# Loading a gated delta-rule kernel in 128-token pieces: large loads, 128-row transposes, on-chip spreads and shared PSUM banks

## The chip, the cores and the metric

One Trainium2 chip, one core. The metric is the device time of one execution in microseconds (us). The kernel before takes 416.6 us (median of 4 runs, 415.4 to 418.9). PE is the matrix engine, PEld its weight loads, DVE the vector engine, ACT the scalar engine, POOL the general engine, SP the engine that here only issues transfers. "SPq" is SP's queue. All runs are on one core; runs called slow by their own set (over 1.5% above the fastest run of the same kernel) are left out of the ratios; the medians are over all four runs.

## The reference

A recurrence over 768 tokens for 32 heads (4 batches of 8, 48 wide), then a two-layer MLP on the 3072 x 384 result.

```python
    k_n = k / (np.linalg.norm(k, axis=-1, keepdims=True) + 1e-06)
    state = np.zeros((B, H, D, D), dtype=np.float32)
# ... cut
    for t in range(S):
        kt, vt, bt = (k_n[:, :, t].copy(), v[:, :, t].copy(), beta[:, :, t, None].copy())
        readout = np.einsum('bhd,bhde->bhe', q[:, :, t], state)
        y[:, :, t] = g[:, :, t] * readout
        v_old = np.einsum('bhde,bhd->bhe', state, kt)
        state = state + bt[:, :, :, None] * np.einsum('bhd,bhe->bhde', kt, vt - v_old)
# ... cut; the MLP: h = x @ w_in; (h+1)^2/4 between -1 and 1, h above, 0 below; @ w_out
```

q, k, v and g lie in memory as [batch, head, token, 48] in float32, so that the 48 numbers of one head and one token, 192 bytes, are the longest run that stays together when tokens lie on the partitions and heads beside each other.

## The kernel before

Both kernels do the recurrence in 24 steps of 32 tokens, and four steps form a group. In a group all that does not need the state is prepared: k is normalised and scaled, k and q are transposed on PE, Gram blocks are formed, a 32 x 32 triangular system is solved for each head and step ("the solve", about 15 us of small operations on POOL, for group 0 on DVE), and two rounds of small matmuls merge the solution. Then the four steps run one after the other, each ending in the *state eviction*, a copy of the state out of PSUM by ACT. The MLP of a group runs on PE beside the next groups. The evictions are the clock by which this text tells the time: s0 is the first, s4 the first of group 1, s22 the last (the prediction and the expectations say "step 4" where this text says s4).

The loads of the kernel before, four transfers of 48 KB per tensor and step, all on SP for groups 1 to 5:

```python
    def load_step(nm, s, eng="SP", prio=0.0):
        p, c = s // 2, s % 2
        t = raw[nm](p)
        for h4 in range(4):
            a = bass.AP(tensor=src[nm].tensor, offset=src[nm].offset + h4 * S * D + s * C * D,
                        ap=[[D, C], [HS, J], [1, D]])
            e = {"SP": nc.sync, "ACT": nc.scalar}[eng]
            P(eng, 0.49, lambda h4=h4, a=a, e=e: e.dma_start(out=t[32 * h4:32 * h4 + 32, c, :, :], in_=a),
              w=[raw[nm].key(p, c, h4)], prio=prio, late=0.33)
# ... cut
    def loads(gi):
        for nm in "kqvg":
            for c in range(GS):
                load_step(nm, gi * GS + c, "SP", at((gi - 2) * GS) + (c + "kqvg".index(nm) * 0.5) * T)
```

The transposes, 64 rows at a time, and most of the small matmuls have this form (Gram blocks shown):

```python
                for jj in range(4):
                    for a in range(2):
                        for r in range(2):
                            rr = slice(64 * r, 64 * r + 64)
                            nc.tensor.matmul(tp[rr, jj, a], kq[rr, c, 4 * half + jj, a, :], i64[rr, :], ...)
# ... cut
            for j in range(J):
                for hh in range(2):
                    for r in range(2):
                        h4 = 2 * r + hh
                        rk = slice(64 * r, 64 * r + D)
                        nc.tensor.matmul(gp[32 * h4:32 * h4 + 32, j], kt[rk, j, 0, 32 * hh:32 * hh + 32], ...)
```

The order of instructions on each engine is decided when the kernel is built, by a list scheduler in the kernel. It has assumed durations for every operation (the second argument of `P`), priorities (`prio`), and one more rule that becomes important below: it counts PE instructions and plans no block of 256 sooner than 3.4 us after the one before. This is an assumption in the code; what the traces show of it comes with the profile after.

```python
            if o["n"]:
                fetch[0] += o["n"]
                while fetch[0] >= 256:
                    fetch[0] -= 256
                    fetch[1] = max(fetch[1] + 3.4, t)
                    end = max(end, fetch[1])
```

Of the kernel before, what the change touches and what calls it, by code (L numbers as in the profile page):

```python
# [22 lines left out]
class Plan:  # L23
# [3 lines left out]
    def __init__(self):  # L27
        self.ops, self.writer, self.readers = [], {}, {}
        self.banks, self.slot = {}, {}

    def add(self, eng, us, fn, r=(), w=(), prio=0.0, ninstr=0, late=0.0, take=None, give=None):
        i = len(self.ops)
        deps = set()
# [16 lines left out]
    def order(self):  # L50
# [10 lines left out]
        out = []  # L61
# [10 lines left out]
        blocked = {}  # L72
        spare = {p: list(range(n)) for p, n in self.banks.items()}
        back = []
        while len(out) < len(ops):
# [8 lines left out]
            if back and (best is None or back[0][0] <= best[0]):  # L84
                t, p, n = heapq.heappop(back)
                spare[p].append(n)
                for e, i in blocked.pop(p, ()):
                    avail[i] = max(avail[i], t)
                    heapq.heappush(ready[e][0], (avail[i], ops[i]["prio"], i))
                continue  # L90
# [8 lines left out]
            if o["take"]:  # L99
                bp = o["take"][0]  # L100
                if not spare[bp]:
                    blocked.setdefault(bp, []).append((e, i))
                    continue
                self.slot[o["take"]] = spare[bp].pop(0)
# [30 lines left out]
def kernel(  # L135
# [11 lines left out]
    nc = tc.nc  # L147
    B, H, S, D = q.shape
# [9 lines left out]
    HS = 4 * S * D  # L158
# [18 lines left out]
    raw = {nm: Ring(f"raw_{nm}", 5 if nm == "g" else 3, [128, 2, J, D], FP) for nm in "kqvg"}  # L177
    src = dict(k=k, q=q, v=v, g=g)
    ksq = Ring("ksq", 2, [128, 2, J, D], FP)
    nsq, nrm, nre, rcp, rs = (Ring(n, 2, [128, 2, J], FP) for n in ("nsq", "nrm", "nre", "rcp", "rs"))  # L180
    kqs = Ring("kq", 5, [128, 2, J, 2, 64], F16)
    vts = Ring("vt", 4, [128, 2, J, D], F16)
    kts = Ring("kt", 8, [128, J, 2, 64], F16)
    bms = Ring("bm", 2, [128, GS, J, 2, 32], F16)
# [14 lines left out]
    rls = Ring("rl", 3, [128, NT], FP)  # L199
    mxs = Ring("mx", 2, [128, NT], FP)  # L200
    r2s = Ring("r2", 2, [128, NT], FP)
    gts = Ring("gt", 23, [128, NT], F16)
# [3 lines left out]
    sb = pool.tile([128, NG, J, GS], FP, name="sb")  # L206
    sps = ps.tile([128, 2, 512], FP, name="sps")
    banks = {}
    for p, n in (("n", 3), ("h", 2), ("o", 1)):
        banks[p] = [ps.tile([128, 512], FP, name=f"ps{p}{i}") for i in range(n)]  # L210
        plan.banks[p] = n
# [7 lines left out]
    def bv(vid, *dims):  # L219

        d, stride = [], 1
        for n in reversed(dims):
            d.insert(0, [stride, n])
            stride *= n
        return _ap(banks[vid[0]][plan.slot[vid]], d)


    braw = pool.tile([128, NG, C], FP, name="braw")
    bt = pool.tile([128, NG, C], FP, name="bt")
    ones = pool.tile([128, 64], FP, name="ones")  # L230
    id32 = pool.tile([128, 32], FP, name="id32")
    i16 = pool.tile([128, 32], F16, name="i16")
    i64 = pool.tile([128, 64], F16, name="i64")
# [3 lines left out]
    eye = pool.tile([128, 2, 16, 16], FP, name="eye")  # L237
    c_half = pool.tile([128, 1], FP, name="c_half")

    def P(eng, us, fn, r=(), w=(), prio=0.0, ninstr=0, late=0.0, take=None, give=None):  # L240
        plan.add(eng, us, fn, r, w, prio, ninstr, late, take, give)

    def load_step(nm, s, eng="SP", prio=0.0):
        p, c = s // 2, s % 2
        t = raw[nm](p)
        for h4 in range(4):
            a = bass.AP(tensor=src[nm].tensor, offset=src[nm].offset + h4 * S * D + s * C * D,
                        ap=[[D, C], [HS, J], [1, D]])
            e = {"SP": nc.sync, "ACT": nc.scalar}[eng]
            P(eng, 0.49, lambda h4=h4, a=a, e=e: e.dma_start(out=t[32 * h4:32 * h4 + 32, c, :, :], in_=a),  # L250
              w=[raw[nm].key(p, c, h4)], prio=prio, late=0.33)

    def rawkeys(nm, p, cs):
        return [raw[nm].key(p, c, h4) for c in cs for h4 in range(4)]

    def beta_load():
        for h4 in range(4):
            for j in range(J):
                a = bass.AP(tensor=beta.tensor, offset=beta.offset + h4 * S + j * 4 * S,
                            ap=[[C, GS], [GS * C, NG], [1, C]])  # L260
                p = 32 * h4 + 4 * j
                P("ACT" if j % 2 else "SP", 0.33, lambda p=p, a=a, e=(nc.scalar if j % 2 else nc.sync): e.dma_start(out=braw[p:p + 4, :, :], in_=a),
                  w=[("braw", p)], prio=-50, late=0.03)

    def setup():
        P("POOL", 0.2, lambda: nc.gpsimd.memset(ones[:], 1.0), w=["ones"], prio=-100)

        def diag():
# [8 lines left out]
            for r2 in range(2):  # L277
                r = slice(64 * r2, 64 * r2 + 64)
                nc.gpsimd.affine_select(out=i64[r, :], in_=ones[r, :], compare_op=ALU.is_equal, fill=0.0,
                                        base=0, pattern=[[-1, 64]], channel_multiplier=1)  # L280
        P("POOL", 2.2, diag, r=["ones"], w=["id32", "upf", "i64"], prio=-99)
        P("DVE", 0.2, lambda: nc.vector.memset(c_half[:], 0.5), w=["c_half"], prio=-100)
        for i in range(kqs.n):
# [365 lines left out]
```

## Time and profile before

| | before |
|---|---|
| time, median (lowest to highest), us | 416.6 (415.4 to 418.9) |
| span of the profiled execution, us | 414.2 |
| first state eviction s0, us | 63.9 |
| s0 to s4 | 66.8 |
| the four groups s4 to s20 | 52.1, 52.9, 51.1, 48.9 |
| s20 to s22 | 21.3 |
| from s22 to the end | 57.2 |

These lines are from the page of the profile of the kernel before: busy time of each engine with its share of the span and its number of instructions; then PE, its granted clock and the DMA engines in 40 slices of the span, as tenths; the queues with packets, MB and the time that the packets took, as a share of 16 engines' span; and the first line of the chain of waits, which is followed back from the last instruction.

```profile
PE 264.4 (64%) x7536; PEld 158.1 (38%) x7536; DVE 216.5 (52%) x357; ACT 160.5 (39%) x277; POOL 182.2 (44%) x284
...
PE   0004145673656569985984897669983499769665
...
PEclk9999655577555666956797899968998589999989
DMA  8995444444554444544434431000100001001001
...
q1 hardware_dynamic: 104000, 22.88, 27.3%
q0 software_dynamic: 2752, 3.15, 4.8%
...
q8 instruction: 59, 0.97, 1.0%
...
PE 26%; SPq 23%; POOL 20%; issue 9%; DMA 9%; DVE 8%; ACT 3%; ACTq 0%; POOLq 0%
```

No engine is full on average. The largest thing that is not work is SP's queue, 23% of the chain. What it does is in the timeline of SP between s0 and s4 (start, duration of the stretch, line, transfer, number of issues): four issues of 48 KB take 1.9 to 3.4 us, one stretch follows the other without a pause.

```profile
72.55 3.41 SPq L250 DMA_DIRECT2D raw_k_61<-in_k_dram  x4
76.06 2.77 SPq L250 DMA_DIRECT2D raw_v_67<-in_v_dram  x4
78.87 1.93 SPq L250 DMA_DIRECT2D raw_q_64<-in_q_dram  x4
```

And these are state evictions s0, s3 and s4 in the timeline of ACT (start, duration, then what the idle time before it ended with):

```profile
63.87 0.80 ACT L494 CAST s_125<-sps 128x768 f16<-128x768 f32 x1 [0.72 <-PE sps L491]
...
81.80 0.80 ACT L494 CAST s_126<-sps 128x768 f16<-128x768 f32 x1 [0.78 <-PE sps L491]
130.72 0.80 ACT L494 CAST s_125<-sps 128x768 f16<-128x768 f32 x1
```

Between s3 and s4 the recurrence stands still for 49 us. Note also the row q8, kind "instruction": it moved 59 packets, 16,384 bytes each by the packet records. 7,536 matmuls and as many weight loads are 15,072 PE instructions, 255.5 for each of these packets; what that means is read from the trace after the change, below.

### The profile page before, as it was taken

To read this page: it belongs to the slowest core of one execution; us is meant where nothing else is said; L and a number is where in the kernel's file an instruction comes from. 1 tells how busy PE (TensorE), PEld (TensorE's weight loads), DVE (VectorE), ACT (ScalarE), POOL (GpSimd) and SP (SyncE) were. 2 spreads that over 40 slices of the span, in tenths; PEclk is the share of its full clock that TensorE was granted. 3 is DMA by queue.
4 is the path that set the end of the run, shared out by engine and by line. 5 is a ranking of instruction groups with operands and counts; after the bars stand their busy time and mean duration, and the time that the engine had idled before them with its cause. 6 is when DMAs were issued, how large, how long until landed. Compare 5 with 4: busy or idle time off the path is not lost.

```text
span 414.2 us, 16889 instructions
## 1 busy us (share of the span) xinstructions
PE 264.4 (64%) x7536; PEld 158.1 (38%) x7536; DVE 216.5 (52%) x357; ACT 160.5 (39%) x277; POOL 182.2 (44%) x284
## 2 busy tenths in 40 slices
PE   0004145673656569985984897669983499769665
PEld 0004034531225235653552464435542355425222
DVE  8303854365433364663984529472493453875530
ACT  0004013342325333452672356525453264555531
POOL 8703062244896338953489526851038420212110
PEclk9999655577555666956797899968998589999989
DMA  8995444444554444544434431000100001001001
GB/s 141 164 156 93 88 92 76 73 87 89 100 99 84 84 83 97 122 90 83 83 69 93 98 95 24 3 3 21 60 6 2 3 22 59 3 2 57 19 20 59
DMA packets 111625, 27.95 MB, mean 67 GB/s; under 512 B 106048, under 2 KB 111168, under 8 KB 111552
## 3 DMA queue, kind: packets, MB, share of 16 engines
q1 hardware_dynamic: 104000, 22.88, 27.3%
q0 software_dynamic: 2752, 3.15, 4.8%
q10 hardware_dynamic: 4800, 0.84, 1.1%
q8 instruction: 59, 0.97, 1.0%
q14 instruction: 14, 0.11, 0.1%
HBM read 25.26 MB, written 4.72 MB: 72 GB/s over the span
## 4 chain that ended last, share of the span: by engine, by line
PE 26%; SPq 23%; POOL 20%; issue 9%; DMA 9%; DVE 8%; ACT 3%; ACTq 0%; POOLq 0%
SPq L250 23%; PE pso_173 L558 11%; POOL tm_108 L401 7%; POOL lm_107 L404 7%; PE psh_172 L530 5%; DMA braw<-in_beta_dram 5%; PE psh_171 L530 3%; POOL lowl_109 L406 2%; DVE lt_106 L393 1%; DMA raw_q_64<-in_q_dram 1%; POOL r_136 L544 1%; DMA raw_k_62<-in_k_dram 1%; ACT rl_133 L533 1%; DVE mx_134 L537 1%; ACT r_137 L547 1%
## 5 line engine op out<-in xcount | busy, mean ns | idle before, releaser
L530 PEld LDWEIGHTS <-win 128*128 128x128 f16 x288 | 27.2, 105 | 64.9 <-issue 47.8
L530 PE MATMUL psh_172<-xt_129,win 128*128 128x512 f16 x69 | 23.2, 454 | 19.8 <-DVE gt_143 L549 8.1
L401 POOL TENSOR_TENSOR tm_108<-lt_106,lm_107 128x30 f32<-128x30 f16 (+7 forms) x75 | 29.9, 399 | 12.0 <-DVE lt_106 L393 6.0
L404 POOL TENSOR_TENSOR lm_107<-lm_107,tm_108 128x30 f32<-128x30 f32 (+7 forms) x75 | 29.2, 390 | 5.9
L365 PE MATMUL psn_168<-i_179,kq_87 64*64 64x64 f16 x96 | 3.3, 221 | 43.2 <-POOL kq_87 L344 36.2
L530 PE MATMUL psh_171<-xt_129,win 128*128 128x512 f16 x75 | 24.6, 443 | 4.4 <-DVE gt_149 L549 2.2
L544 POOL TENSOR_TENSOR r_136<-rl_132 128x512 f32<-128x512 f32 x8 | 9.3, 1158 | 37.6 <-ACT rl_132 L533 37.6
L530 PE MATMUL psh_172<-xt_130,win 128*128 128x512 f16 x63 | 20.3, 437 | 7.5 <-DVE gt_160 L549 1.6
L530 PE MATMUL psh_171<-xt_130,win 128*128 128x512 f16 x81 | 23.6, 402 | 2.0 <-DVE gt_151 L549 1.8
L544 POOL TENSOR_TENSOR r_136<-rl_133 128x512 f32<-128x512 f32 x8 | 8.3, 1043 | 33.0 <-ACT rl_133 L533 33.0
L365 PEld LDWEIGHTS <-kq_87 64*64 64x64 f16 x192 | 5.3, 135 | 44.3 <-POOL kq_87 L344 36.2
L533 ACT ACTIVATE rl_133<-psh_171,c_half 128x512 f32<-128x512 f32 x19 | 13.0, 685 | 18.6 <-POOL r_136 L544 10.6
L544 POOL TENSOR_TENSOR r_136<-rl_131 128x512 f32<-128x512 f32 x8 | 8.3, 1040 | 23.2 <-ACT rl_131 L533 23.2
L533 ACT ACTIVATE rl_131<-psh_172,c_half 128x512 f32<-128x512 f32 x17 | 11.7, 687 | 14.5 <-PE psh_172 L530 14.5
L533 ACT ACTIVATE rl_131<-psh_171,c_half 128x512 f32<-128x512 f32 x15 | 10.4, 690 | 16.5 <-POOL r_136 L544 11.0
L533 ACT ACTIVATE rl_132<-psh_171,c_half 128x512 f32<-128x512 f32 x18 | 12.3, 686 | 7.6 <-PE psh_171 L530 7.4
L430 PE MATMUL psn_169<-l_112,bm_105 32*32 32x32 f16 x256 | 4.3, 227 | 16.2 <-DVE l_112 L411 16.2
L533 ACT ACTIVATE rl_132<-psh_172,c_half 128x512 f32<-128x512 f32 x14 | 9.7, 690 | 12.5 <-PE psh_172 L530 12.2
L333 DVE TENSOR_REDUCE nsq_78<-ksq_76 128x16 f32<-128x768 f32 x6 | 5.7, 950 | 15.4 <-POOL ksq_76 L331 15.4
L335 ACT ACT_TABLE_LOAD x1 | 1.3, 1283 | 30.6 <-DMA raw_q_65<-in_q_dram 30.6
L430 PEld LDWEIGHTS <-bm_105 32*32 32x32 f16 x384 | 6.1, 115 | 17.9 <-issue 17.8
L411 DVE STREAM_TRANSPOSE l_112<-lowl_109 128x1024 f16<-128x1024 f16 x3 | 3.7, 1245 | 17.2 <-POOL lowl_109 L406 17.2
(473 smaller groups left out, 808.8 us busy)
## 6 DMA issues: line engine op xcount, KB each, us to landing
wout<-in_moe_w_out_dram POOLq DMA_DIRECT2D x4, 384.0 KB, 8.4
raw_v_67<-in_v_dram SPq DMA_DIRECT2D x32, 48.0 KB
raw_v_68<-in_v_dram SPq DMA_DIRECT2D x32, 48.0 KB
raw_k_63<-in_k_dram SPq DMA_DIRECT2D x32, 48.0 KB
raw_q_66<-in_q_dram SPq DMA_DIRECT2D x32, 48.0 KB
raw_v_69<-in_v_dram SPq DMA_DIRECT2D x32, 48.0 KB
out_dram<-ot_161 SPq DMA_DIRECT2D x8, 192.0 KB
out_dram<-ot_162 SPq DMA_DIRECT2D x8, 192.0 KB
```

The costliest lines, as they stand in the source:

```text
L250: P(eng, 0.49, lambda h4=h4, a=a, e=e: e.dma_start(out=t[32 * h4:32 * h4 + 32, c, :, :], in_=a), w=[raw[nm].key(p, c, h4)], prio=prio, lat ...
L333: P("DVE", 1.0, lambda: nc.vector.tensor_reduce(out=nsq(p)[:], in_=ksq(p)[:], axis=AX.X, op=ALU.add), r=[ksq.key(p)], w=[nsq.key(p)], prio ...
L365: nc.tensor.matmul(tp[rr, jj, a], kq[rr, c, 4 * half + jj, a, :], i64[rr, :], start=(jj == 0 and a == 0), stop=True, skip_group_check=True)
L393: P("DVE", 1.95, lambda: nc.vector.transpose(out=lt[:].rearrange("p i j -> p (i j)"), in_=_ap(bm, [[1, 32], [64, 32]])), r=[bms.key(gi, c) ...
L401: e.tensor_tensor(out=tv, in0=_ap(lt, [[528, 2], [32, n], [0, j + 1]], 32 * (j + 1) + j), in1=_ap(lm, [[256, 2], [0, n], [1, j + 1]], 16 * ...
L404: e.tensor_tensor(out=lv, in0=lv, in1=tv, op=ALU.subtract)
L406: P(eng, 0.61, lambda: e.tensor_copy(out=_ap(lowl(gi), [[528, 2], [1, 16], [32, 16]]), in_=lm[:]), r=[lms.key(gi)], w=[lowl.key(gi)], prio ...
L430: nc.tensor.matmul(ep[r, c, j], bm[r, off + c, j, 0, :], l16[r, :, (off + c) * J + j], start=False, stop=True, skip_group_check=True)
L530: nc.tensor.matmul(hp, win[:, kt_, m * 128:m * 128 + 128], xt[:, kt_].rearrange("p b t -> p (b t)"), start=(kt_ == 0), stop=(kt_ == 2))
L533: P("ACT", 0.69, lambda: nc.scalar.activation(out=rl[:], in_=bv(n, NT), func=AF.Relu, bias=c_half[:], scale=0.5), r=[n, "c_half"], w=[rls. ...
L544: P("POOL", 1.05, lambda: nc.gpsimd.tensor_tensor(out=r2[:], in0=rl[:], in1=rl[:], op=ALU.mult), r=[rls.key(i)], w=[r2s.key(i // 2)], prio ...
L558: nc.tensor.matmul(bv(n, DM), gts(gi * NM + m)[:, b * GS * C:(b + 1) * GS * C], wout[:, m, :], start=(m == 0), stop=(m == NM - 1))
```

## The change

The intent is to take the issue load off SP and work off POOL. k, v, q and g of a whole group (128 tokens, 32 heads) come in one to two transfers each, with tokens on the 128 partitions. k and v are scaled in that layout, g and q are cast by their transfers on POOL's queue, and k and q are transposed by 128 x 128 matmuls. The steps need 32 tokens of four heads on the partitions, so g, v and k are put together in one tile and *spread* by four SBUF-to-SBUF transfers a step. The PSUM banks, which were split 3, 2 and 1 among uses, form one pool of six. In addition the k squares go from POOL to ACT, the MLP's middle function is split differently over the engines, and the raw k and v tiles, the scaled k and the q tile are single buffers. The 32 loads of beta, of which 16 hold SP's queue from 5.7 to 22.8 us in the kernel before, become four on ACT's queue; this, too, bears on s0.

```diff
-    raw = {nm: Ring(f"raw_{nm}", 5 if nm == "g" else 3, [128, 2, J, D], FP) for nm in "kqvg"}
+    kraw = Ring("kraw", 1, [128, NH, D], FP)
+    vraw = Ring("vraw", 1, [128, NH, D], FP)
+    ks = Ring("k", 1, [128, NH, 64], F16)
+    qs = Ring("q", 1, [128, NH, 64], F16)
+    pks = Ring("pk", 2, [128, NH, KW], F16)
+    kvs = Ring("kv", 7, [128, J, KW], F16)
 ... cut
-    for p, n in (("n", 3), ("h", 2), ("o", 1)):
-        banks[p] = [ps.tile([128, 512], FP, name=f"ps{p}{i}") for i in range(n)]
+    plan.nbanks = 6
+    banks = [ps.tile([128, 512], FP, name=f"psn{i}") for i in range(6)]
+    plan.limits = {"n": (6, 0), "h": (3, 1), "o": (2, 1)}
 ... cut
+    def whole(t, g, a=0, n=NH):
+        return bass.AP(tensor=t.tensor, offset=t.offset + g * GS * C * D + a * S * D, ap=[[D, GS * C], [S * D, n], [1, D]])
+    def load_k(g, prio, parts):
+        for a, n in parts:
+            P("SP", 0.3 + 0.08 * n, lambda a=a, n=n: nc.sync.dma_start(out=kraw(g)[:, a:a + n], in_=whole(k, g, a, n)),
+              w=[kraw.key(g, a)], prio=prio, late=2.7 * n / NH)
+    def load_q(g, prio):
+        P("POOL", 2.0, lambda: nc.gpsimd.dma_start(out=qs(g)[:, :, 0:D], in_=whole(q, g)), w=[qs.key(g)], prio=prio, late=2.7)
 ... cut
+    def spread(s, keys, prio):
+        g, c = s // GS, s % GS
+        for h4 in range(4):
+            P("SP", 0.46, lambda h4=h4: nc.sync.dma_start(
+                out=kvs(s)[32 * h4:32 * h4 + 32, :, :],
+                in_=pks(g)[32 * c:32 * c + 32, :, :].rearrange("p (j a) w -> p a j w", a=4)[:, 2 * (h4 % 2) + h4 // 2]),
+              r=keys, w=[kvs.key(s, h4)], prio=prio, late=0.33)
 ... cut
-                            nc.tensor.matmul(tp[rr, jj, a], kq[rr, c, 4 * half + jj, a, :], i64[rr, :],
+                    nc.tensor.matmul(tp[:, hh, 0], kk[:, o:o + 128], i128[:], start=(hh == 0), stop=True, skip_group_check=True)
+                    nc.tensor.matmul(tp[:, hh, 1], qq[:, o:o + 128], i128[:], start=False, stop=True, skip_group_check=True)
```

## The prediction

> **What bounds the kernel now.** The chain of waits gives its largest share, 23%, to the SyncE queue at the line that issues the q, k, v, g loads: 384 loads of 48 KB, all but 16 on SyncE. The timeline of that queue shows 0.48 us each at best (1.93 us for four), often 2.8 to 3.2 us for four, without a pause until 251 us of the 414 us span. The 32 beta loads hold the SyncE and ACT queues for 17 and 19 us. So the first state eviction (ACT, 796 ns) comes at 63.9 us, and from step 3 (81.8 us) to step 4 (130.7 us) the recurrence waits 49 us for the second group. Groups of four steps after that take 52, 53, 51 and 49 us. The last had no load pressure left (DMA share 1% to 12% after 260 us): PE is busy 61% to 98% of each 20 us window, the rest is in-order waits, above all the triangular solve on POOL (about 15 us), its casts (one 2.41 us) and what follows. After the last state eviction (357 us) come 57 us of MLP, two PSUM banks, about 3 us for two tiles.
>
> **What the change does.** By the instruction order of both kernels SyncE goes to 18 large loads, 96 SBUF-to-SBUF spreads and 24 stores; q and g go to the POOL queue with a cast. [...] The 98,000 packets of 192 B stay; spreads add 24,600 of 288 B. By the queue table (104,000 packets, 27.3% of 16 engines' span) a packet takes 1.1 ns of all 16: 18 us per group of loads, 5 us of spreads. That fits under a 40 us group, but not under the start, where two groups and the weights saturate DMA. [...]
> PE: 768 transposing 64x64 matmuls become 192 of 128x128, 25 us become perhaps 15. POOL loses ksq (18 us), the q copies (10 us) and the slow cast, and gains 12 descriptor generations (estimate 2 us each, scaled from the weight loads' 0.55 and 0.77 us) and 6 squares. ACT gains 11 us of squares. DVE loses two MLP operations a group.
>
> **On the critical path.** First state eviction at about 45 us (-19); the solve to there stays 20 us. First group 38 us instead of 67 (-29). Later groups 43 us instead of 51 (-32 over four): PE about 38 us busy per group, others 30 to 33. Tail 48 instead of 57, with three MLP and two output banks (-9). Sum -90 to -95.
>
> **Prediction: 322 us, 298 to 350. Faster by over 2%: 0.96; within 2%: 0.02; slower: 0.02.**
>
> **What would show it.** Chain of waits: SyncE queue below 5%, PE or POOL first. First state eviction at 40 to 50 us; no gap above 25 us between state evictions; groups of 39 to 47 us; PE busy 235 to 255 us; mean clock 0.82 to 0.9; about 130,000 packets.
>
> **What would make it wrong.** Single buffers for raw k and v, k and q tie loads, POOL scaling, spreads and solve into one ring; in-order SyncE may hold a spread behind a load that waits for POOL. [...] If groups stay at 50 us, 350 us; near PE-bound, 298.

What it calls descriptor generations are POOL's DMA_DIRECT2D instructions: an estimated 2 us each there, 1.78 us for q and 1.74 for g in the profile after. The transposes, put at 25 us before and perhaps 15 after, keep PE busy for 23.6 and 21.1 us in the two traces.

## The result, and the profile after

| | before | predicted | after |
|---|---|---|---|
| time, median, us | 416.6 | 322 (298 to 350) | 352.5 (350.7 to 353.7) |
| s0 | 63.9 | 45 | 53.7 |
| s0 to s4 | 66.8 | 38 | 52.9 |
| four groups, s4 to s20 | 204.9 | 172 (43 each) | 178.5 (41.6, 45.3, 48.8, 42.8) |
| s20 to s22 | 21.3 | (no change) | 18.1 |
| from s22 to the end | 57.2 | 48 | 47.6 |
| mean granted clock | 0.805 | 0.82 to 0.9 | 0.864 |

The kernel is faster, by a ratio of 0.845 (95% interval 0.840 to 0.850), and 2.5 us slower than the upper end of the predicted range. A ratio here is the mean time of one kernel's fast runs over that of the other's in the same rounds, so it is not quite the ratio of the medians quoted. The result is correct. About 30 us of the expected gain are missing. By stages of the span it is 27: 9 in s0, 15 in the first group, 6 or 7 in the later groups, less the 3 that s20 to s22 gave unexpectedly. Most of the rest lies in the prediction's own sum: its four terms (-19, -29, -32, -9) make -89 and so 327.6 us, not the -90 to -95 and 322 that it states.

The same lines of the page of the profile after:

```profile
PE 249.5 (71%) x6960; PEld 154.2 (44%) x6960; DVE 223.2 (64%) x359; ACT 168.0 (48%) x292; POOL 166.4 (47%) x253
...
PE   0240323546675978459889789797996989999986
...
PEclk9999999855855785659978899698998799999999
DMA  9999999974789206977349103012210001001102
...
q0 software_dynamic: 52096, 7.87, 30.7%
q1 hardware_dynamic: 74896, 20.46, 29.3%
...
q8 instruction: 54, 0.88, 1.0%
...
PE 45%; issue 15%; POOL 13%; DMA 12%; DVE 11%; ACT 3%; ACTq 1%; DVEq 0%; POOLq 0%; SPq 0%
```

SP's queue is gone from the chain and PE is first, as predicted. What was not predicted is the 15% named "issue", time in which an engine waited for nothing that the profile shows. The packets are as many as predicted (132,000), but their time grew: 27.3% and 4.8% of 414.2 us were 133 us of 16 engines before, 30.7% and 29.3% of 350.9 us are 211 us now. A packet of the load queue cost 0.273 x 414.2 us / 104,000 = 1.1 ns before and costs 0.293 x 350.9 us / 74,896 = 1.4 ns now, and one of the POOL queue 2.1 ns. But these averages mix kinds of packets, and they invite a wrong reading, that the crowd made every packet dearer. The packet records in the packed traces (`trace.npz`; mean ns of one packet on one of the 16 engines, so 16 ns is 1.0 ns of all 16) take the kinds apart:

| packets | before | after, first 40 us | after, 110 to 180 us | after, 180 to 260 us |
|---|---|---|---|---|
| 192 bytes, SP's queue | 16 | 22 | 17 | none |
| 192 bytes, ACT's queue | 16 | 28 | none | none |
| 288 bytes, the spreads | none | 33 | 24 | 23 |
| 192 bytes cast to 96, POOL's queue (q and g) | none | 28 | 29 | 29 |

The crowd of the first 40 us (the row of nines) adds 6 to 12 ns to the uncast packets. A packet that is cast on POOL's queue takes 28 to 29 ns everywhere, also between 180 and 260 us, where the DMA engines are mostly below half busy.

Evictions s0, s3 and s4 after:

```profile
53.73 0.80 ACT L541 CAST s_110<-sps 128x768 f16<-128x768 f32 x1 [3.28 <-PE sps L538]
...
82.65 0.80 ACT L541 CAST s_111<-sps 128x768 f16<-128x768 f32 x1 [0.94 <-PE sps L538]
106.67 0.80 ACT L541 CAST s_110<-sps 128x768 f16<-128x768 f32 x1 [1.87 <-PE sps L538]
```

Now the timeline of PE from 64 to 78 us. Each line is a run of equal matmuls (start, duration, shape, xcount), each of which has a weight load that is not shown here; the brackets tell the idle time before it and what ended it.

```profile
64.55 0.34 PE L409 MATMUL psn_150<-kt_86 48*32 48x64 f16 x23
69.08 0.32 PE L409 MATMUL psn_150<-kt_86 48*32 48x64 f16 x9 [4.19 <-issue]
69.18 0.64 PE L409 MATMUL psn_152<-kt_86 48*32 48x64 f16 x32
69.75 0.52 PE L538 MATMUL sps<-u_109,kv_79 32*48 32x48 f16 x32
70.20 0.50 PE L557 MATMUL psn_153<-u_109,bm_88 32*32 32x48 f16 x32
71.25 0.43 PE L496 MATMUL psn_149<-s_111,kt_85 48*32 48x48 f16 x23 [0.54 <-ACT s_111 L541]
74.18 0.28 PE L496 MATMUL psn_149<-s_111,kt_85 48*32 48x48 f16 x9 [2.50 <-issue]
```

PE stops in the middle of a block of 32 equal, independent matmuls: 23 of them, a hole of 4.19 us, the other 9. Between this hole and the next, in the same place of another block, are 9 + 32 + 32 + 32 + 23 = 128 matmuls, with their weight loads 256 instructions. The packets of q8 fit that size: 54 for 13,920 PE instructions here, 257.8 for each, and 255.5 in the kernel before. So this text takes a packet of q8 for a *block* of 256 instructions of PE's program, and its arrival for a *refill*. PE consumed the block in 2.6 us (69.08 to 71.7) and then waited, so the two starts lie 5.1 us apart. That the waits are refills can be read from the packet records of q8: each of the 21 waits ends 1.3 to 1.6 us after a block of 16,384 bytes has landed, the one at 69.08, for instance, 1.44 us after 67.64. In a quiet stretch late in the same trace, with the DMA engines at 0 to 2 tenths, the period is shorter but still there:

```profile
264.05 0.22 PE L557 MATMUL psn_153<-u_108,bm_89 32*32 32x48 f16 x7 [0.76 <-issue]
...
267.50 0.27 PE L496 MATMUL psn_149<-s_110,kt_86 48*32 48x48 f16 x14 [0.71 <-issue]
...
270.96 0.45 PE L473 MATMUL psn_153<-l_97,bm_90 32*32 32x32 f16 x18 [1.30 <-issue]
```

That is 3.45 us from refill to refill at rest, and up to 6.5 us elsewhere (146.29 to 152.76). By the packet records a block takes 0.9 to 1.4 us to move in either case; where one long wait follows another it starts 2.5 to 4.1 us after the end of the first, at rest 1.1 us. Whether the crowd causes this late start isn't shown: it also occurs in e6 below, with a third of the packets. Summed over the trace, PE's waits of this kind are 37.0 us (21 of them, the longest 4.3) after the change, and 12.4 us (18, the longest 2.2) before it. Three of those before, in the timeline of PE, with the same spacing:

```profile
61.37 0.78 PE L442 MATMUL psn_168<-x_113,e_116 32*32 32x32 f16 x41 [1.01 <-issue]
...
64.83 0.27 PE L510 MATMUL psn_170<-u_123,bm_104 32*32 32x48 f16 x9 [0.65 <-issue]
...
68.28 0.31 PE L491 MATMUL sps<-u_124,kq_87 32*64 32x48 f16 x9 [0.38 <-issue]
```

A third thing in the trace concerns DVE on the way to s0. Two of its operations take eight to ten times as long as their like, each while POOL scales v (16.66 to 19.66 and 32.28 to 35.12 us). This is the timeline of DVE:

```profile
13.53 0.35 DVE L354 COPY pk_76<-k_74 128x768 f16<-128x768 f16 x1
...
17.07 2.81 DVE L354 COPY pk_76<-k_74 128x768 f16<-128x768 f16 x1
...
32.53 2.72 DVE L441 TENSOR_TENSOR tm_93<-lt_91,lm_92 128x112 f32<-128x112 f16 x1
```

That the two wait for POOL is read from the times: they start 0.41 and 0.25 us after POOL's scaling has begun and end 0.22 and 0.13 us after it has ended, whereas an operation that DVE had begun at 16.07, before POOL, took 0.96 us like its twin at 11.79. How POOL holds DVE up is not shown. DVE loses 4.9 us to them before s0.

So there were four suspects for the missing 30 us: the crowd of 192-byte packets (theory A), POOL's order and the single buffers (theory B), the preparation of group 1 standing in line behind group 0 in the order fixed at the build (theory C), and PE's refills (theory D; theory A had the refills as a victim of the crowd).

### The profile page after: what moved, and what is told of

The parts are those of the page before. It is cut to its first block, busy times and chain, and to the rows that moved or that the text cites. A ratio compares the mean times of both kernels' runs of the same rounds, so it can differ in the third digit from the quotient of the medians.

```text
span 350.9 us, 15376 instructions
## 1 busy us (share of the span) xinstructions
PE 249.5 (71%) x6960; PEld 154.2 (44%) x6960; DVE 223.2 (64%) x359; ACT 168.0 (48%) x292; POOL 166.4 (47%) x253
## 2 busy tenths in 40 slices
DMA packets 132000, 30.17 MB, mean 86 GB/s; under 512 B 126432, under 2 KB 131552, under 8 KB 131936
## 3 DMA queue, kind: packets, MB, share of 16 engines
q0 software_dynamic: 52096, 7.87, 30.7%
q1 hardware_dynamic: 74896, 20.46, 29.3%
## 4 chain that ended last, share of the span: by engine, by line
PE 45%; issue 15%; POOL 13%; DMA 12%; DVE 11%; ACT 3%; ACTq 1%; DVEq 0%; POOLq 0%; SPq 0%
DMA kraw_61<-in_k_dram 7%; PE psn_150 L604 4%; POOL lm_92 L444 3%; PE psn_149 L577 3%; PE psn_153 L577 3%; POOL tm_93 L441 3%; PE psn_154 L604 3%; PE psn_150 L577 2%; PE psn_152 L604 2%; PE psn_154 L577 2%; PE psn_149 L604 2%; DMA kv_79<-pk_76 2%; PE sps L538 2%; PE psn_151 L577 2%; PE psn_151 L604 1%
## 5 line engine op out<-in xcount | busy, mean ns | idle before, releaser
L590 POOL TENSOR_TENSOR rl_117<-rl_117 128x512 f32<-128x512 f32 x12 | 13.6, 1135 | 40.8 <-ACT rl_117 L580 40.8
L444 POOL TENSOR_TENSOR lm_92<-lm_92,tm_93 128x28 f32<-128x28 f32 (+6 forms) x70 | 25.7, 367 | 5.5
L441 POOL TENSOR_TENSOR tm_93<-lt_91,lm_92 128x28 f32<-128x28 f16 (+6 forms) x70 | 24.5, 349 | 5.1
L590 POOL TENSOR_TENSOR rl_119<-rl_119 128x512 f32<-128x512 f32 x6 | 6.6, 1099 | 30.9 <-ACT rl_119 L580 30.9
L383 PEld LDWEIGHTS <-k_74 128*128 128x128 f16 x96 | 12.6, 133 | 19.6 <-DVE k_74 L351 14.6
L340 ACT ACTIVATE ksq_63<-kraw_61 128x768 f32<-128x768 f32 x12 | 10.1, 840 | 18.4 <-DMA kraw_61<-in_k_dram 18.4
L590 POOL TENSOR_TENSOR rl_116<-rl_116 128x512 f32<-128x512 f32 x6 | 6.2, 1041 | 19.4 <-ACT rl_116 L580 19.4
L384 PEld LDWEIGHTS <-q_75 128*128 128x128 f16 x96 | 12.5, 130 | 4.0 <-issue 2.7
L541 ACT CAST s_111<-sps 128x768 f16<-128x768 f32 x11 | 8.8, 797 | 10.6 <-PE sps L538 10.5
L262 POOL DMA_DIRECT2D q_75<-in_q_dram x6 | 10.7, 1776 | 6.7 <-PE psn_153 L384 3.4
L541 ACT CAST s_110<-sps 128x768 f16<-128x768 f32 x12 | 9.6, 798 | 8.7 <-PE sps L538 8.7
L383 PE MATMUL psn_149<-i_160,k_74 128*128 128x128 f16 x20 | 4.5, 271 | 12.8 <-DVE k_74 L351 12.8
L351 POOL TENSOR_TENSOR k_74<-kraw_61,rs_72 128x768 f16<-128x768 f32 x4 | 5.8, 1474 | 15.9 <-DMA kv_79<-pk_77 15.2
L432 POOL TENSOR_SCALAR lm_92<-lt_91 128x512 f32<-128x512 f16 x5 | 7.5, 1496 | 10.3 <-DVE lt_91 L422 10.2
L359 POOL TENSOR_TENSOR pk_77<-vraw_62,sb 128x1536 f16<-128x1536 f32 x3 | 8.4, 2787 | 7.9 <-DMA vraw_62<-in_v_dram 7.9
L590 POOL TENSOR_TENSOR rl_118<-rl_118 128x512 f32<-128x512 f32 x6 | 6.8, 1138 | 10.8 <-ACT rl_118 L580 10.8
L359 POOL TENSOR_TENSOR pk_76<-vraw_62,sb 128x1536 f16<-128x1536 f32 x3 | 8.6, 2864 | 6.8 <-DMA vraw_62<-in_v_dram 6.8
L577 PE MATMUL psn_149<-xt_114,win 128*128 128x512 f16 x33 | 11.0, 448 | 0.0
```

The lines of the kernel that those rows point to most:

```text
L262: P("POOL", 2.0, lambda: nc.gpsimd.dma_start(out=qs(g)[:, :, 0:D], in_=whole(q, g)), w=[qs.key(g)], prio=prio, late=2.7)
L340: P("ACT", 0.25 + 1.3 * f, lambda hs=hs: nc.scalar.activation(out=ksq(g)[:, hs], in_=kr[:, hs], func=AF.Square), r=[kraw.key(g, a)], w=[ks ...
L359: P(eng, (0.15 + 1.65 * f) if eng == "DVE" else (0.2 + 2.8 * f), lambda hs=hs, a=a, n=n, eng=eng: EW[eng].tensor_tensor(out=pk[:, hs, D:2 ...
L383: nc.tensor.matmul(tp[:, hh, 0], kk[:, o:o + 128], i128[:], start=(hh == 0), stop=True, skip_group_check=True)
L384: nc.tensor.matmul(tp[:, hh, 1], qq[:, o:o + 128], i128[:], start=False, stop=True, skip_group_check=True)
L432: e.tensor_scalar(out=_ap(lm, [[256, nb], [16, 16], [1, 16]], om), in0=_ap(lt, [[528, nb], [32, 16], [1, 16]], ot), scalar1=-1.0, scalar2= ...
```

## The experiments

All are edits of the changed kernel unless said otherwise, each beside runs of the kernel before on the same chip. The last row of the table is the changed kernel again, on the chip of e9 to e11.

| run | correct | median us | ratio to before, 95% interval |
|---|---|---|---|
| changed kernel | yes | 352.5 | 0.845 (0.840 to 0.850) |
| e1_small_weights | no | 347.7 | 0.830 (0.822 to 0.838) |
| e2_weights_later | yes | 355.3 | 0.848 (0.840 to 0.857) |
| e4_k_first | yes | 351.2 | 0.835 (0.825 to 0.845) |
| e5_banks321 | yes | 356.2 | 0.850 (0.843 to 0.856) |
| e6_long_rows | no | 345.0 | 0.823 (0.812 to 0.833) |
| e3_split_v | yes | 353.2 | 0.849 (0.842 to 0.856) |
| e7_before_two_queues (edit of before) | yes | 403.4 | 0.969 (0.960 to 0.977) |
| e8_k_first_split_v | yes | 350.7 | 0.841 (0.834 to 0.848) |
| e9_kraw2 | yes | 349.9 | 0.839 (0.832 to 0.845) |
| e10_group1_early | yes | 354.8 | 0.853 (0.844 to 0.862) |
| e11_group1_earlier | yes | 350.3 | 0.840 (0.833 to 0.846) |
| e13_rows_and_early | no | 336.2 | 0.803 (0.796 to 0.810) |
| e15_early_v_after | yes | 350.8 | 0.838 (0.830 to 0.846) |
| e17_half_instr | no | 328.7 | 0.786 (0.780 to 0.792) |
| e18_half_instr_rows | no | 316.0 | 0.758 (0.753 to 0.763) |
| e19_half_with_nops | no | 678.5 | 1.618 (1.605 to 1.632) |
| e20_half_columns | no | 353.1 | 0.844 (0.836 to 0.851) |
| e12_after_again | yes | 355.3 | 0.852 (0.845 to 0.859) |

### Was the kernel before bound by SP's issues?

e7_before_two_queues:

```diff
-                load_step(nm, gi * GS + c, "SP", at((gi - 2) * GS) + ...
+                load_step(nm, gi * GS + c, "ACT" if c % 2 else "SP", at((gi - 2) * GS) + ...
```

> The kernel before, with the loads of groups 1 to 5 alternately on the SyncE and the ACT queue instead of all on SyncE; same packets, correct result. If the kernel before was short of issue time on SyncE: the SyncE queue's share of the chain falls from 23% to under 10%, step 3 to step 4 takes under 35 us instead of 49, total 380 to 400 us (ACT pays for 184 issues). If it was short of packet time on the DMA engines: step 3 to step 4 stays at 45 to 49 us and the total within 2% of before.

Measured: 403.4 us, 3% faster. The SP queue left the chain:

```profile
PE 36%; POOL 18%; DMA 14%; DVE 14%; issue 11%; ACT 5%; ACTq 1%; SPq 0%; POOLq 0%; DVEq 0%
```

So SP was indeed what the chain ran through, but step 3 to step 4 still took 41.5 us (95.2 to 136.8), and s4 came 6 us later than in the kernel before; the gain lies after s4 (262.8 instead of 283.5 us). SP's share of 23% was 95 us of the chain, and taking it away with the packets unchanged (111,624, and 111,625 before) was worth 13. ACT, which also evicts the state, pays for the issues that it took over (three times between 96 and 124 us four of them took 1.8 to 2.1 us on its queue), so this is no clean measure of SP's issues alone. The expectation of 380 to 400 was too good: the share of 95 us was not a gain of 95, because the next waits stood close behind (DMA at 14% of the chain and DVE at 14%, 9% and 8% before).

### The start, one suspect at a time

e1_small_weights loads about a sixteenth of `w_in` and a quarter of `w_out`; e2_weights_later keeps the weights whole and issues them after group 1's transposes.

```diff
-  out=win[32 * h4 + p0:32 * h4 + p0 + n, kt, :], in_=moe_w_in[r0:r0 + n, :]),
+  out=win[32 * h4 + p0:32 * h4 + p0 + n, kt, 0:128], in_=moe_w_in[r0:r0 + n, 0:128]),
 ... e2 instead:
-  after=[kts.key(0, J - 1)], w=[("win", h4, kt, p0)], prio=prio, late=0.6)
+  after=[kts.key(1, J - 1)], w=[("win", h4, kt, p0)], prio=prio, late=0.6)
```

> The changed kernel, same order of instructions, but the weight loads bring only one sixteenth of w_in and a quarter of w_out, which the matmuls then use again and again (a wrong result on purpose): about 5.1 MB less to read in the first 60 us. Theory A (the start is short of DMA: it delays the second group's k, the spreads and the refills of PE's instructions): stalls of PE by issue before 90 us fall from 14.6 to at most 7 us, first state eviction from 53.7 to at most 50 us, that of step 4 from 106.7 to at most 95 us, total 335 to 343 us. Theory B (the ring of single buffers with in-order POOL and SyncE holds the second group, whatever the DMA load): step 4 stays within 4 us of 106.7, total at least 348 us.

> The changed kernel with all weight loads put after the transposes of the second group (right result). Theory A: the second half of the second group's k lands before 33 us instead of 38.4, step 4's state eviction by 98 us instead of 106.7, total 340 to 347 us; the MLP of the first group may start later, its weights land only near 75 us. Theory B: total 349 to 355 us.

e4_k_first lets group 2's g load and v scaling on POOL wait for group 1's k scaling; e5_banks321 gives the PSUM banks back to their old limits.

```diff
+        plan.writer[("kdone", g)] = plan.writer[ks.key(g, 16)]
-              r=[vraw.key(g), "sb"], w=[pks.key(g, "v", a)], prio=prio + 1)
+              r=[vraw.key(g), "sb"], w=[pks.key(g, "v", a)], prio=prio + 1, after=[("kdone", g - 1)] if g == 2 else ())
 ... and the same for g's load; e5 instead:
-    plan.limits = {"n": (6, 0), "h": (3, 1), "o": (2, 1)}
+    plan.limits = {"n": (3, 0), "h": (2, 0), "o": (1, 0)}
```

> The changed kernel; only for the third group, POOL issues the g load and scales v after it has scaled the second group's k (right result). Theory B: POOL scales that k at about 51 us instead of 57.8, step 4's state eviction comes 5 to 8 us earlier than 106.7, total 343 to 348 us. Theory A: the k scaling moves, but refills and DMA stay as they are and step 4 gains at most 3 us, total 350 us or more.

> The changed kernel with the PSUM banks limited as before, 3 for the recurrence, 2 for the MLP input, 1 for the output (right result). If the shared banks brought the shorter tail and a part of the shorter groups: the time after the last state eviction goes from 47.6 back to 54 to 58 us, groups get 2 to 4 us longer, total 362 to 375 us. If the banks do not matter beside the loads: at most 357 us.

Measured: e1 brings s0 to 50.4 and s4 to 99.9 us, with no later gain. e2 brings s0 to 50.1, but s4 comes 1 us later, at 107.7. e4 brings s4 from 106.7 to 99.9 and the profiled span from 350.9 to 345.7, though its runs spread (347.5 to 354.0, the last slow). Each is worth 0 to 2% and leaves most of the 30 us. e5 shows that the banks are part of the tail, as predicted: from s22 to the end 54.0 us instead of 47.6; the total is only 3.7 us higher and not 10 to 22, because s20 to s22 was 1.9 us shorter and the run of groups between s12 and s20 4.7 us shorter (86.9 instead of 91.6), where 2 to 4 us more per group were expected.

e3_split_v cuts POOL's v scaling into four, and e8_k_first_split_v joins that with e4.

```diff
-            keys, kk = prep(g, t0, [(a, n, "POOL") for a, n in HALVES], [(0, NH, "POOL")])
+            keys, kk = prep(g, t0, [(a, n, "POOL") for a, n in HALVES], [(8 * i, 8, "POOL") for i in range(4)])
```

> The changed kernel with each v scaling on POOL cut from one operation of 32 heads (2.8 us) into four of 8 heads; correct result. If a DVE operation that starts while POOL runs such a scaling has to wait until it ends: the two DVE operations before the first state eviction that took 2.81 and 2.72 us instead of 0.35 and 0.28 take at most 1.0 us each, the first state eviction comes 3 to 5 us earlier (49 to 51 us), the total falls by 2 to 6 us. If the long DVE operations have another cause, they stay over 2 us and the first state eviction stays at 53 to 54 us.

> The changed kernel with both POOL changes at once: group 2's g load and v scaling after group 1's k scaling (which alone brought step 4 from 106.7 to 99.9 us) and each v scaling in four operations; correct result. If the POOL order and the DVE operations behind the v scaling are two separate costs: step 4 at 94 to 98 us, total 340 to 345 us, faster than the changed kernel by 2 to 3%. If one absorbs the other: step 4 at 98 to 101 us, total 345 to 350 us.

Measured: the long DVE operations get shorter, as they should if they wait for POOL. These lines are the same two kinds of operation in the timeline of DVE of e3:

```profile
16.82 0.36 DVE L354 COPY pk<-k 128x768 f16<-128x768 f16 x1
...
34.06 0.83 DVE L441 TENSOR_TENSOR tm<-lt,lm 128x52 f32<-128x52 f16 x1
34.93 0.76 DVE L444 TENSOR_TENSOR lm<-lm,tm 128x52 f32<-128x52 f32 x1
35.72 0.72 DVE L441 TENSOR_TENSOR tm<-lt,lm 128x28 f32<-128x28 f16 x1
```

But four short stretches of the solve (0.72 to 0.83 us, where the same operations take 0.19 to 0.21 in the changed kernel) replace one long one, so most of that loss stays. The copy of 0.36 us proves nothing: it began 0.08 us before POOL's first piece (16.90). In e8 it began after it and took 0.94 us, not 2.81, which supports the wait. s0 comes at 51.9, 1.8 us earlier and not 3 to 5. This is hardly the cut's doing: e4 and e5, with v scaled in one piece, also have s0 at 51.9, and there too the copy slipped in before POOL (at 16.58 and 16.67). The total did not move, and e8 missed too (s4 at 105.3).

### Packets

e6_long_rows reads k, v and q as contiguous rows, so that the same bytes come in far fewer packets (42,900 in all instead of 132,000), and a quarter of g (3.5 MB less to read). So it takes away bytes as well as packets; e1, which reads 5.3 MB less of the weights in nearly as many packets (130,464), gained 2%.

```diff
+    def rows(t, g, a=0, n=NH):
+        return bass.AP(tensor=t.tensor, offset=t.offset + g * GS * C * NH * D + a * D, ap=[[NH * D, GS * C], [1, n * D]])
-  in_=whole(k, g, a, n)
+  in_=rows(k, g, a, n)
 ... v and q alike; g:
-  nc.gpsimd.dma_start(out=pks(g)[:, :, 0:D], in_=whole(g_in, g))
+  nc.gpsimd.dma_start(out=pks(g)[:, 0:8, 0:D], in_=whole(g_in, g, 0, 8))
```

> The changed kernel, but k, v and q are loaded as contiguous rows of 6 KB (3 KB after the cast) instead of 192-byte pieces, same bytes and same issues, and g loads only 8 of 32 heads; wrong result on purpose. Theory A (the start and the first group are short of DMA because of the small packets, and the PE instruction refills wait in that crowd): PE issue waits before 100 us fall from about 20 us to under 8 us, the first state eviction comes at 45 to 49 us instead of 53.7, step 4 at 82 to 92 us instead of 106.7, total 320 to 335 us. Theory B (in-order POOL with single buffers): the first state eviction at 51 to 54 us, step 4 not before 98 us, total 343 to 352 us.

Measured: 345.0 us. Two of its four runs, the profiled one among them, were slow, so its steps are only hints; the ratio of the fast runs is 0.823 where the changed kernel has 0.845 and 0.852. Taking away two thirds of the packets is worth about 3%, 9 to 12 us, and not 17 to 32 as theory A wanted. Nor did the refill waits go with the crowd: before 100 us they are 12.8 us in its trace against 14.6 in the changed kernel (the expectation's "about 20" is too high).

### The order of group 1's preparation

Another reading of the start: in the changed kernel and in e1 to e6 and e8 s4 follows the start of group 1's k scaling on POOL by 46 to 59 us (57.8 to 106.7 in the changed kernel). That scaling waits for k's norm, which stands on DVE behind the whole first solve (until 42 us). e9 gives k a second buffer; e10 and e11 also give group 1's preparation a priority ahead of the first solve; e12 is the changed kernel once more (355.3 us, above the 348 to 354 expected of it, so two measurements of one kernel differ by 0.8%).

```diff
-    kraw = Ring("kraw", 1, [128, NH, D], FP)
+    kraw = Ring("kraw", 2, [128, NH, D], FP)
 ... e10 (-30) and e11 (-44):
-        t0 = at((g - 1) * GS) - 1.0 * T
+        t0 = at((g - 1) * GS) - 1.0 * T if g != 1 else -30
```

> The changed kernel with a second buffer for raw k alone, so group 1's k is loaded at once instead of waiting for group 0's scaling; correct result. Theory C (step 4 comes some 47 to 52 us after POOL starts group 1's k scaling, and that start is held by in-order queues: group 1's norm stands behind the whole first triangular solve on DVE, which ends at 42 us): group 1's first k scaling starts no earlier than 42 us, step 4 at 90 to 102 us, total 338 to 348 us. Theory A (the late landing of k, 38 us, is what holds it): the k scaling starts at 25 to 35 us, step 4 at 80 to 88 us, total 322 to 335 us.

> The second buffer for raw k, and group 1's preparation (norm, scaling, transposes, Gram blocks, solve) given a priority ahead of the first solve's operations on DVE; correct result. Theory C: the k scaling of group 1 starts at 22 to 34 us, the first state eviction stays at 50 to 57 us, step 4 follows at 76 to 90 us instead of 106.7, total 318 to 335 us. Theory A: with all of the packets and the refill waits still there, step 4 stays over 96 us and the total over 340 us.

> As the run before it, with a still earlier priority for group 1's preparation, so that its Gram blocks and solve also go ahead of the first solve. Theory C: step 4 at 74 to 88 us, the first state eviction up to 5 us later than in that run, total 318 to 338 us and within 2% of it. Theory A: as there.

> The changed kernel itself, unaltered, on the same chip as the three above, so that they can be set against it: 348 to 354 us, ratio to before 0.84 to 0.85.

Measured, in the profiled executions:

| | changed | e9 | e10 | e11 | e15 |
|---|---|---|---|---|---|
| group 1's first k scaling on POOL | 57.8 | 60.1 | 27.4 | 24.3 | 27.3 |
| s0 | 53.7 | 64.2 | 63.9 | 67.1 | 64.2 |
| s4 | 106.7 | 113.1 | 107.7 | 111.8 | 110.8 |
| s20 | 285.2 | 282.4 | 282.6 | 282.0 | 280.6 |
| span | 350.9 | 349.0 | 349.1 | 348.5 | 347.3 |

In e10, e11 and e15 the scaling did come 30 us earlier, and s4 did not. Theory C falls as a cause that stands alone. s0 came 10 to 13 us later, probably because the earlier load of k pushed v and q of the first groups back in the crowd (in e11 a q load is on the chain for 16 us and a v load for as long); no run tests this. The striking thing is the row s20. It lies within 5 us in all five, whether s4 came at 107 or at 113. Something paces the groups that none of these edits touched.

### Packets and order together, or PE's refills?

e13_rows_and_early joins e6 and e11. e15_early_v_after is e10 with group 2's v scaling held back until group 1's solve is done. e17_half_instr joins pairs of small matmuls, so that one instruction does the columns of two (the second head of the pair gets the wrong weights); e18_half_instr_rows adds the long rows.

```diff
-            for j in range(J):
+            for j in range(0, J, 2):
 ...
-  nc.tensor.matmul(gp[32 * h4:32 * h4 + 32, j], kt[rk, j, hh, 0, c], kt[rk, j, hh, :, c],
+  nc.tensor.matmul(gp[32 * h4:32 * h4 + 32, j:j + 2], kt[rk, j, hh, 0, c], kt[rk, j:j + 2, hh, :, c],
 ... alike in the merges and in the four matmul loops of a step; e15:
-  r=[vraw.key(g), "sb"], w=[pks.key(g, "v", a)], prio=prio + 1)
+  r=[vraw.key(g), "sb"], w=[pks.key(g, "v", a)], prio=prio + 1, after=[lowx.key(1, 0)] if g == 2 else ())
```

> Long rows (as e6_long_rows) together with the second k buffer and the early order of group 1 (as e11_group1_earlier); wrong result on purpose. If packets and order hide each other: the first state eviction at 46 to 54 us, step 3 before 75 us, step 4 before 88 us, total 318 to 335 us. Theory D (from the first steps on PE is the limit, by its busy time and the refill of its instruction buffer after every 256 instructions): step 4 may come early, but the later groups take longer in return, step 20 comes no earlier than 272 us and the total is 336 to 346 us.

> The changed kernel with pairs of small matmuls (32 and 48 rows) joined into one of twice the columns: 7,900 PE instructions instead of 13,900, the same columns, order and data movement; wrong result on purpose. Theory D: PE's waits named issue fall from 37 us to under 12 us, the first state eviction comes at 46 to 50 us, step 4 at 92 to 100 us, and the total is 318 to 336 us. Theories A and C (DMA packets or in-order preparation): the waits turn into waits for DVE, POOL and DMA, total 342 to 352 us.

> Half the PE instructions and long rows together; wrong result on purpose. If the two costs are separate, total 308 to 328 us and at least 6 us under e17_half_instr; if the packets cost time only through the refill of PE's instructions, within 4 us of e17_half_instr.

> As e10_group1_early (second k buffer, group 1's preparation ahead of the first solve on DVE), and group 2's v scaling on POOL only after group 1's solve, which it held up to 77 us there; correct result. Theory C: group 1's solve starts on POOL before 62 us, step 4 at 88 to 100 us, total 335 to 345 us. Theory D: whatever step 4 does, step 20 comes at 278 to 286 us and the total is 344 to 352 us.

Measured: e17 takes 328.7 us, 24 less than the changed kernel. These are lines of its page:

```profile
PE 237.1 (72%) x3936; PEld 138.6 (42%) x3936; DVE 219.9 (67%) x359; ACT 167.6 (51%) x292; POOL 167.2 (51%) x253
...
q8 instruction: 31, 0.51, 0.7%
...
PE 39%; DVE 20%; DMA 18%; POOL 12%; issue 5%; ACT 4%; SPq 1%; ACTq 1%; DVEq 0%; POOLq 0%
```

31 refills instead of 54, and PE's issue waits fall from 37.0 to 4.6 us. These two are all that the table of waits has left of them (total, times, longest), and both end 1.4 to 1.5 us after a block landed:

```profile
PE psn L557 <- issue: 2.5, 1, 2.5
...
PE psn L496 <- issue: 2.1, 1, 2.1
```

By steps:

| | predicted | changed | e17 | e18 |
|---|---|---|---|---|
| s0 | 45 | 53.7 | 46.8 | 49.2 |
| s0 to s4 | 38 | 52.9 | 54.8 | 42.0 |
| s4 to s20 | 172 | 178.5 | 162.8 | 157.2 |
| s20 to s22 | 21.3 | 18.1 | 17.8 | 17.8 |
| s22 to the end | 48 | 47.6 | 47.5 | 47.6 |
| span | | 350.9 | 329.7 | 313.8 |

With the refills halved, s0 comes where it was predicted and the later groups are shorter than predicted; the first group is not better (s4 came at 101.6, where 92 to 100 was expected). With the packets gone too, e18 has it at 42.0, and takes 316.0 us; long rows alone have it at 46.1, in the profile of e6 that is only a hint. The two costs add up: long rows are worth about 9 to 12 us with the full program and 12.7 us (328.7 to 316.0) with the halved one. Where the chain of e17 had 18% DMA, that of e18 has 6%:

```profile
q1 hardware_dynamic: 32016, 20.46, 25.0%
q0 software_dynamic: 9856, 6.10, 14.7%
...
DVE 32%; PE 32%; POOL 15%; issue 9%; DMA 6%; ACT 4%; ACTq 1%; SPq 0%; DVEq 0%; POOLq 0%
```

e13 took 336.2 us, a ratio of 0.803 against 0.823 for the long rows alone. Its s4 came at 101.6 and not before 88, and its s20 at 269.6 (theory D had said not before 272), so packets and order hid each other only in small part, and the pacing remained. e15 did what theory D said: whatever happened at the start (s4 at 110.8), s20 came at 280.6 and the median is 350.8.

### Instructions, or PE's work?

e17 also halves the weight loads, and PE's busy time fell by 12.4 us, from 249.5 to 237.1. So 24 us could be partly that. e19_half_with_nops put two empty instructions behind each joined matmul.

```diff
+    def mm2(*a, **kw):
+        nc.tensor.matmul(*a, **kw)
+        for _ in range(2):
+            nc.tensor.nop(nofuse=True, hint='x')
```

> e17_half_instr with two empty instructions on PE's queue after each joined matmul, so that PE has 13,900 instructions again but still only half of the small matmuls and weight loads; wrong result on purpose. If the instruction count costs the time (a refill after each 256): PE's issue waits of up to 4 us are back, over 25 us in all, and the total is 343 to 356 us, as the changed kernel. If it was the matmul and weight-load work: the total stays at 325 to 334 us. In between says how much belongs to each; the empty instructions' own issue time would push it up too, and the trace shows it as many short gaps instead of few long ones.

Measured: 678.5 us, outside everything expected. 6,048 empty instructions cost about 350 us over e17, 58 ns each on average, at a lower granted clock (0.682), so the run does not tell what refills cost. It is inconclusive. Two things in it fit all the same: q8 again moved 54 blocks, for 7,872 + 6,048 = 13,920 instructions, and PE, which now needs over 12 us for a block (676.5 / 54), waited for none of them. e20_half_columns turns the question round: all instructions and weight loads stay, and the small matmuls do half of their columns.

```diff
-  nc.tensor.matmul(up[r, j], z[r, j], rr[r, j],
+  nc.tensor.matmul(up[r, j, 0:24], z[r, j], rr[r, j, 0:24],
 ... alike in the other loops, and the six banks zeroed once at the start
```

> The changed kernel with every small matmul working on half of its columns (16 or 24 instead of 32 or 48, gram 32 instead of 64), the PSUM banks zeroed once at the start; instruction count, weight loads, order and transfers as in the changed kernel; wrong result on purpose. If the refill after every 256 instructions costs the time: PE's issue waits stay at 30 to 45 us, a smaller PE busy time (by 8 to 25 us) goes into them and other waits, and the total is 343 to 354 us. If it was PE's work: total 322 to 336 us. [...]

Measured: 353.1 us, and in its page:

```profile
PE 237.5 (68%) x6960; PEld 143.2 (41%) x6960; DVE 224.1 (64%) x365; ACT 167.9 (48%) x292; POOL 166.9 (48%) x253
...
q8 instruction: 54, 0.88, 1.1%
...
PE 43%; DVE 16%; issue 15%; POOL 11%; DMA 6%; SPq 4%; ACT 3%; DVEq 0%; POOLq 0%; ACTq 0%
```

PE's busy time fell just as in e17 (237.5 against 237.1 us), the 54 refills stayed, and the total did not move: 353.1 us, between the two measurements of the changed kernel (352.5 and 355.3). PE's issue waits rose from 37.0 to 45.1 us; what was saved in work was waited for instead. So the 24 us of e17 belong to the number of PE's instructions, and the same saving in PE's work alone is worth little or nothing here (zeroing the six banks can hide an estimated 2.7 us, six times half of the 0.91 us that DVE's memset of 128x1024 takes in the changed kernel's trace). e17 halves weight loads together with matmuls, and e20 keeps both; that it is the fetch and not the weight loads is read from the waits, which fall by 32 us and all end 1.3 to 1.6 us after a block lands. Nor is it the clock, which was 0.895 to 0.921 in e17's runs and 0.864 to 0.887 in the changed kernel's: in e11 a run at 0.838 took 351.4 us and three at 0.931 to 0.936 took 349.7 to 350.4.

No correct version is better than the changed kernel by 2%: the best of them by the ratio, e4_k_first, has an interval that touches the changed kernel's first measurement. e9 and e11 are the nearest to a gain: all their runs (349.0 to 351.4) lie under all of e12 on the same chip (354.2 to 357.5), by 1.5%, but not under the changed kernel's first measurement. The experiments point to fewer PE instructions, but a correct kernel with half of them needs another layout of the small matmuls and was not built. It stays open.

## Why the prediction was right and wrong

**What bounds the kernel before: right, with a caveat.** The SP queue was on the chain for 23%, and after the change it is at 0%. e7, which moves half of the later issues to ACT without the rest of the change, gained 13 us of the 95 us which that share looks like.

**What would show it: mostly right.** SP's queue below 5% (0%), PE first in the chain (45%), no gap above 25 us between evictions (24.0 from s3 to s4), PE busy 249.5 us in 235 to 255, clock 0.864 in 0.82 to 0.9, 132,000 packets. Two of the marks missed: s0 at 53.7 and not 40 to 50, and one later group at 48.8 with 47 as the upper end (another, at 41.6, lay in the range).

**The tail: right.** 48 predicted, 47.6 measured, and e5, which gives the banks back, has 54.0: the banks are 6.4 of the 9.6 us gained.

**"First state eviction at about 45 us (-19)": wrong by 8.7 us.** The step that failed was to shift s0 by the time saved in loading and keep the 20 us after it. Two costs were not in it. With half of PE's instructions s0 comes at 46.8 (e17): PE stood still for 4.0 us until 48.2 and for 2.4 us until 53.3, waiting for instructions. And DVE lost 4.9 us behind POOL's v scaling, which POOL now does in one operation of 2.8 us; in e3, e4 and e5, where one of the two delays happened not to occur, s0 came at 51.9, 1.8 us earlier.

**"First group 38 us instead of 67 (-29)": wrong by 14.9 us, the largest part.** The prediction saw that two groups and the weights saturate DMA at the start (the engines are 90% or more busy in the first eight slices after the change, 70 us), said so, and put no number to it. It took 1.1 ns for every load packet from a profile in which none was cast. The packets of q and g, half of the loads, are now cast on POOL's queue and take 28 to 29 ns on one engine instead of 16, in the crowd or out of it. By these figures a group's loads are an estimated 23 us of 16 engines and not 18, and all packets together took 211 us instead of 133 (the spreads, which the prediction had counted, are about 37 of it). How much of the 14.9 us this caused is not shown. e18 shows what is gained with both things gone, the refills and the packets: the group then takes 42.0 us, 54.8 without the refills alone. For the remaining 4 us e18's trace has a candidate that no run tests: between s3 and s4 two copies of k on DVE take 6.5 us together, behind two operations of POOL, and stand on the chain for 6.4. How POOL's order shares in it (e4 brought s4 7 us earlier in its trace) was not settled.

**"Later groups 43 us instead of 51: PE about 38 us busy per group": the size was nearly right, the reason not.** They took 44.6 on average. PE was busy for 36.7 us per group, about as predicted, but of the other 8 us 5 were instruction waits, which the prediction did not have: from s4 to s20 PE waited 20.2 us for nothing but instructions. That the size came out close is luck. With most of those waits gone the groups take 40.7 (e17).

**The missing term, then, is PE's instruction refill.** Halving the instructions saves 24 us of the total (e17 against the changed kernel, with e20 as the control), and long rows save 9 to 13 us (e6, and e18 against e17). Their sum is more than the 30 us between 322 and 352, because the later groups then come out shorter than predicted (157.2 us against 172). The refills were there before as well, 59 of them, five more than now, and cost 12.4 us of PE's waits, it seems because PE stood waiting for loads anyway and the next block arrived meanwhile (read from the trace, not tested). With the load wait gone, PE ran through a block in 2.6 us (69.08 to 71.7) where blocks came 3.45 us apart at rest. The prediction could have known: the scheduler in both kernels has the rule of 3.4 us for 256 instructions in plain sight, the trace before has holes of that spacing at 61, 65 and 68 us, and the change takes away only 1,152 of 15,072 PE instructions.

**What the chances said.** Faster by over 2% had 0.96, and that happened. The list of what would make it wrong named the ring of single buffers and in-order queues. These are real waits in the trace (SP's queue waited 27.0 us in all for POOL's k scaling to free the k buffer, and one k scaling on POOL ended its 15.2 us of idle time with the landing of a spread), but edits that removed them (e9, e10, e11, e15) moved the total by 2% at most.

## What to carry to other kernels

When a change takes away the wait that hides everything else, go through the costs that were hidden: here the standstill before s4 fell from 49 us to 24.0, and PE's waits for instructions rose from 12.4 to 37.0 us. Look for such a cost block by block: 256 instructions that PE ran through in 2.6 us, against holes 3.45 us apart. In a sum over a long stretch it disappears: from s4 to s20 the trace has 4,524 matmuls, with their weight loads 35 blocks, an estimated 122 us at 3.45 us each, which is less than the 146.9 us that PE was busy there, and yet PE waited 20.2 us for instructions. A per-packet cost read from one kind of packet did not hold for another (16 ns became 28 to 29 for those cast on POOL's queue), and less so in a crowd (16 became 22 to 28); a crowd that one has seen needs a number in the sum. And an engine's busy time can fall by 12 us without any gain (e20), while its number of instructions is what costs (24 us, e17): to tell the two apart, cut each by itself, and see in the trace whether the waits move.
